# DeltaNet layer and two-level mixture of experts: chunks of 32 tokens instead of 64, the triangular inverses moved from TensorE to VectorE

## The chip, the core and the metric

The kernel runs on one core of one Trainium2 chip. The metric is the time of the whole program on the device, in microseconds (us); lower is better. Engines are named as in the profile: PE is TensorE (PEld its weight loads), DVE VectorE, ACT ScalarE, POOL GpSimd, SP the queue of SyncE, which issues most DMAs. Everything is fp32.

## What is computed

A DeltaNet layer of 4 batches x 8 heads over 768 tokens of width 48, and a mixture of 16 experts (4 groups of 4) on its result, read as 3072 tokens of width 384:

```python
k_n = k / (np.linalg.norm(k, axis=-1, keepdims=True) + 1e-06)
for t in range(S):                       # S = 768, per batch and head
    y[t] = q[t] @ state                  # state is 48 x 48
    v_old = state.T @ k_n[t]
    state = state + beta[t] * np.outer(k_n[t], v[t] - v_old)
x = y.transpose(0, 2, 1, 3).reshape(B * S, H * D)
g_idx, g_w = argmax and softmax weight of x @ w_group
e_idx, e_w = the same of x @ w_expert[g_idx]
out = (g_w * e_w)[:, None] * (np.maximum(x @ w1[g_idx, e_idx], 0) @ w2[g_idx, e_idx])
```

## The kernel before, in words

**Stage one, the DeltaNet.** The recurrence is cut into 12 chunks of 64 tokens. Two batches lie on the 128 partitions at a time (64 tokens each), so there are 24 units u, two for each chunk. For every chunk a unit lower triangular 64 x 64 matrix, made of the products of the chunk's keys with each other, has to be inverted for each batch and head: 384 matrices in all.

`prepare` (L186) does what needs no state. POOL scales the keys by their norms (L190) and the values (L193), PE turns the scaled keys (L198), ACT copies them (L200), PE forms the products keys x (keys, queries) into `g_ps` (L209), DVE masks them (L213, L218) and POOL makes three more operands of them (L222 to L225). Then the inverse is doubled up in five levels (loop at L231). Each level multiplies on PE into `y_ps` (L239), is masked by DVE (L242), is multiplied twice on PE into `m_ps` (L249, L251), and is copied by ACT (L261; L256 at the last level). Each of these products is 64 x 64 by 64 x 64; the two batches use opposite quarters of the PE array. An fp32 product leaves two records in the trace.

`advance` (L265) brings a unit through the recurrence: `a_ps` (keys x state, L273), `f` (values minus that, DVE, L278), `w_ps` (the inverse times f, L284), `w` (ACT copy, L287), `d_ps` (keys x w, L292), and the state `s_bd` in SBUF is added up by DVE (L299). `outputs` (L303) adds queries x state (L308) and masked products x w (L314) into `o_ps`, and ACT copies them to `x` (L318).

`route` (L345) takes the two units of a chunk: PE turns `x` (L350) and multiplies by the router's weights (L355), DVE and POOL find group, expert and weight in some 30 tiny operations, PE counts ranks (L389, L391), DVE makes one-hot tiles (L418, L421), PE multiplies them into `p_ps` (L423), and DVE adds this to `table` (L424). The rows of `x` go to `x_dram` by SP.

`norms` (L173) makes the norms of all keys from squares on POOL and sums on DVE, at the start. Buffers in PSUM come in pairs (`bufs=2`, L118). What runs when on each engine is decided by a planner from the order of the program text (loop at L427: the two units' `advance`, the next two units' `prepare`, then `route`).

**Stage two, the experts.** From `idx` (L444) POOL gathers the tokens of each expert from `x_dram`, PE multiplies by w1 (L481) and w2 (L488), and POOL scatters the rows to the result (L492). Weights arrive two experts ahead. The change leaves this stage alone.

## Time and profile before

| what | value |
|---|---|
| median of three runs | 1145.88 us (1144.49 to 1146.13) |
| the profiled execution, span from first to last instruction | 1145.2 us |
| busy: PE, PEld, DVE, ACT, POOL | 1026.7, 863.4, 316.1, 226.8, 245.5 us |
| busy shares of PE, PEld, DVE, ACT, POOL | 90%, 75%, 28%, 20%, 21% |
| granted clock of TensorE, mean of the span | 0.955 of 2.4 GHz |
| instructions in the profile | 35577 |

The profiled execution is one run; its own time is its span, and the page records nothing around it. A share of busy time is a mean over two stages with different limits, so the page is read by stage. The views used further down are a table of busy time by stretch (one row for each stretch: length, then busy us and number of instructions for each engine, granted clock, DMA share, GB/s), groups of instructions (line, engine, operation, tiles, shapes, count, then busy us and mean ns of one, then the idle time before them), and the timeline (start us, duration us, engine, line, operation). The clock is 1.00 where TensorE runs at 2.4 GHz and 0.50 where it runs at 1.2 GHz.

### The profile page before, as it was taken

What the parts mean: (1) busy time and instruction counts of PE and PEld (TensorE: products, weight loads), DVE (VectorE), ACT (ScalarE), POOL (GpSimd) and SP (SyncE); (2) the same over time, 40 slices, a digit from 0 to 9 for tenths busy, and PEclk for the clock granted to TensorE, in tenths of its full rate; (3) what the DMA queues carried; (4) which work ended last, traced back from release to release, by engine and by line L of the source; (5) the groups of instructions that cost most, each with busy time, mean ns of one, the idle gap of its engine ahead of it and who ended that gap; (6) DMA issues with size and microseconds to landing.
All of it is one profiled execution on the core that took longest, in us unless ns stands there. A gap on an engine that the chain in (4) does not pass through costs nothing. (4 is left out here: it accounts for less than half of the span.)

```text
span 1145.2 us, 35577 instructions
## 1 busy us (share of the span) xinstructions
PE 1026.7 (90%) x16298; PEld 863.4 (75%) x16298; DVE 316.1 (28%) x983; ACT 226.8 (20%) x429; POOL 245.5 (21%) x389
## 2 busy tenths in 40 slices
PE   0698999999999999998999999978999999999996
PEld 0587888888888887888888888866776677677674
DVE  4533434242423334242334242330100100110010
ACT  0132322222222222222222222210110011011000
POOL 5613122222222222122122221102211211221110
PEclk9999899999999999999999999988999999999998
DMA  9500100000100001010100000003545555464520
GB/s 297 209 11 10 31 17 23 23 24 17 30 17 21 26 17 30 10 30 17 31 9 17 16 17 2 17 16 107 190 146 191 165 185 173 165 199 141 192 68 11
DMA packets 41545, 83.49 MB, mean 73 GB/s; under 512 B 4377, under 2 KB 30156, under 8 KB 41394
## 3 DMA queue, kind: packets, MB, share of 16 engines
q1 hardware_dynamic: 33698, 65.30, 17.8%
q0 software_dynamic: 4096, 11.08, 2.9%
q10 hardware_dynamic: 3600, 4.82, 1.3%
q8 instruction: 128, 2.10, 0.8%
q14 instruction: 23, 0.19, 0.0%
HBM read 71.70 MB, written 11.06 MB: 72 GB/s over the span
## 5 line engine op out<-in xcount | busy, mean ns | idle before, releaser
L239 PE MATMUL y_ps<-mm,at 64*64 64x64 f32 x3840 | 227.7, 229 | 47.0 <-POOL mm L222 41.5
L251 PE MATMUL m_ps<-mm,y 64*64 64x64 f32 x3840 | 248.5, 228 | 0.2
L239 PEld LDWEIGHTS y_ps<-mm,at 64*64 64x64 f32 x3840 | 183.4, 140 | 69.3 <-POOL mm L222 51.9
L251 PEld LDWEIGHTS m_ps<-mm,y 64*64 64x64 f32 x3840 | 223.2, 143 | 2.4 <-DVE y L242 1.2
L249 PE MATMUL m_ps<-y,mm 64*64 64x64 f32 x3072 | 216.2, 233 | 1.3
L249 PEld LDWEIGHTS m_ps<-y,mm 64*64 64x64 f32 x3072 | 195.3, 142 | 16.0 <-DVE y L242 15.2
L242 DVE TENSOR_TENSOR y<-y_ps,con 128x256 f32<-128x256 f32 x240 | 101.8, 424 | 371.7 <-PE y_ps L239 368.7
L261 ACT ACTIVATE mm<-m_ps 128x512 f32<-128x512 f32 x192 | 114.7, 597 | 385.8 <-PE m_ps L251 385.8
L481 PE MATMUL h_ps<-xt,w 128*128 128x256 f32 x768 | 171.6, 384 | 8.1 <-DVE xt L475 8.1
L481 PEld LDWEIGHTS h_ps<-xt,w 128*128 128x128 f32 x768 | 145.9, 192 | 31.2 <-DVE xt L475 11.7
L488 PE MATMUL y_ps<-w,hid 128*128 128x384 f32 x512 | 167.7, 486 | 0.0
L488 PEld LDWEIGHTS y_ps<-w,hid 128*128 128x128 f32 x512 | 97.3, 190 | 64.4
L491 DVE TENSOR_SCALAR yo<-y_ps,xg 128x384 f32<-128x384 f32 x32 | 19.8, 618 | 321.0 <-PE y_ps L488 316.5
L484 ACT ACTIVATE hid<-h_ps 128x512 f32<-128x512 f32 x64 | 38.2, 597 | 322.3 <-PE h_ps L481 322.3
L492 POOL DMA_INDIRECT out_dram<-yo,idx x32 | 32.4, 1012 | 289.9 <-DVE yo L491 285.8
L190 POOL TENSOR_TENSOR kp<-k_all,rs 128x384 f32<-128x384 f32 x24 | 19.8, 829 | 303.9 <-PE g_ps L209 185.8
L209 PE MATMUL g_ps<-kqt 48*64 48x128 f32 x768 | 58.9, 284 | 0.7 <-ACT kqt L200 0.7
L224 POOL TENSOR_TENSOR at<-gq,con 128x256 f32<-128x256 f32 x48 | 34.9, 726 | 77.4 <-DVE gq L213 77.4
L198 PE MATMUL kt_ps<-con,kp 128*128 128x128 f32 x96 | 17.1, 300 | 36.4 <-POOL kp L190 34.8
L209 PEld LDWEIGHTS g_ps<-kqt 48*64 48x64 f32 x768 | 43.0, 137 | 2.3 <-ACT kqt L200 1.1
L284 PE MATMUL w_ps<-f,mt 64*64 64x48 f32 x704 | 43.0, 241 | 0.2 <-DVE f L278 0.2
L273 PE MATMUL a_ps<-s_bd,kqt 128*64 128x96 f32 x352 | 42.4, 262 | 0.0
(115 smaller groups left out, 922.2 us busy)
## 6 DMA issues: line engine op xcount, KB each, us to landing
w<-in_w_dram SPq DMA_DIRECT2D x32, 1536.0 KB, 6.8
x_dram<-x SPq DMA_DIRECT2D x48, 97.0 KB, 2.2
k_all<-in_k_dram ACTq DMA_DIRECT2D x24, 192.0 KB, 4.7
v<-in_v_dram SPq DMA_DIRECT2D x24, 192.0 KB, 2.5
kqt<-in_q_dram SPq DMA_DIRECT2D x48, 96.0 KB, 2.2
con<-in_const_dram SPq DMA_DIRECT2D x1, 708.5 KB, 5.2
xg<-x_dram,idx POOLq DMA_INDIRECT x32, 3.2
out_dram<-yo,idx POOLq DMA_INDIRECT x32, 3.3
```

The source lines that it names most:

```text
L209: nc.tensor.matmul(g_ps[halves[b], j], lhsT=kqt[rows, 0, j, t], rhs=kqt[rows, :, j, t], start=True, stop=True, skip_group_check=True)
L224: nc.gpsimd.tensor_tensor(at, gq[:, :, 0, :], eye, op=ALU.add)
L239: nc.tensor.matmul(y_ps[b, j], lhsT=at[b, j], rhs=mm[b, 0, j], start=True, stop=True, skip_group_check=True)
L242: nc.vector.tensor_tensor(y, y_ps, mask[:, None, :].to_broadcast([128, NP, C]), op=ALU.mult)
L249: nc.tensor.matmul(m_ps[b, 0, j], lhsT=mm[b, 1, j], rhs=y[b, j], start=True, stop=True, skip_group_check=True)
L251: nc.tensor.matmul(m_ps[b, 1, j], lhsT=y[b, j], rhs=mm[b, 1, j], start=True, stop=True, skip_group_check=True)
L261: nc.scalar.activation(new, m_ps, ACT.Copy)
L273: nc.tensor.matmul(a_ps[halves[b], 2 * j:2 * j + 2, :], lhsT=kqt[:, 0, j, halves[b]], rhs=s_bd[:, 2 * g + b, j], start=True, stop=True, sk ...
L284: nc.tensor.matmul(w_ps[b, h], lhsT=mts[h % 2][b, h // 2], rhs=f[b, h], start=True, stop=True, skip_group_check=True)
L481: nc.tensor.matmul(h_ps[:, k], lhsT=w1[:, j, (f + k) * 128:(f + k + 1) * 128], rhs=xt[:, j], start=(j == 0), stop=(j == DC - 1), skip_grou ...
L484: nc.scalar.activation(hid[:, f:f + 2], h_ps, ACT.Relu)
L488: nc.tensor.matmul(y_ps, lhsT=hid[:, f, i * 128:(i + 1) * 128], rhs=w2[:, f], start=(f == 0), stop=(f == FC - 1))
```

## The change

Chunks are 32 tokens long and all four batches lie on the partitions at once (4 x 32 = 128), so there are 24 chunks u in one chain. The changed functions:

- `gram(u)`: PE multiplies raw keys by (keys, queries) in 32 products; ACT copies the key part into `gt`, transposed for the inverse, and the query part into `gq`, which POOL masks. There is no key scaling and no PE turn of keys: keys arrive from HBM in both layouts (`kq`, `kv`).
- `inverse(g)`: for a group of four chunks, DVE transposes 32 x 32 blocks so that each of the 128 partitions holds one whole 32 x 32 matrix (4 chunks x 8 heads x 4 batches = 128). The norms are the root of its diagonal (ACT Ln and Exp). Then 30 column steps follow, j = 1 to 30, each two DVE instructions over (31 - j) x j elements; POOL scales before and after, and DVE transposes back to `mt`.
- `scale(u)`: POOL multiplies the values by the norms.
- `advance(u)`: as before with 32 x 32 inverses. The state stays in PSUM (`s_ps`, four banks), PE accumulates into it, and ACT copies it to `s_bd`.
- `logits(u)` and `route(r)`: the router's scores for each chunk, the rest for each four chunks.
- The order on PE, DVE, ACT and POOL is as written: `work(n)` gives n steps to each unfinished `inverse` and `route` between the parts of `advance`.
- PSUM has single buffers: 4 banks of state, 2 of `g` (`g_ps`, `r_ps`, `p_ps`), 1 of `s` (`a_ps`, `w_ps`, `t_ps`, `l_ps`), 1 of `o`. `norms`, `root` and the masks of the doubling are gone.

The core of the diff (the old `prepare` and `advance` are printed above):

```diff
-C = 64
-LEVELS = (2, 4, 8, 16, 32)
+C = 32
+RG = 4
+LEAD = 9
...
+ps = first.enter_context(tc.tile_pool(name="ps", bufs=1, space=PSUM))
+s_ps = ps.tile([128, B, 512], F32, tag="state", name="s_ps")
+NB, NV = LEAD + 3, 4
...
+def gram(u):
+    g, uu = divmod(u, RG)
+    kqt = kqt_[u % NB]
+    if uu == 0:
+        gts[g] = wk.tile([128, C, RG, H], F32, tag="gt", name=f"gt{g}")
+    g_ps = ps.tile([128, 2, 512], F32, tag="g", name=f"g_ps{u}")
+    g_out = g_ps[:, :, 0:NP * 2 * C].rearrange("p f (j a t) -> p f j a t", j=NP, a=2)
+    for j in range(NP):
+        for b in range(B):
+            for hh in range(2):
+                rows = slice(hh * 64, hh * 64 + D)
+                nc.tensor.matmul(g_out[quads[b], hh, j], lhsT=kqt[rows, 0, j, quads[b]],
+                                 rhs=kqt[rows, :, j, quads[b]], start=True, stop=True,
+                                 skip_group_check=True)
+    nc.scalar.activation(
+        gts[g][:, :, uu].rearrange("p t (f j) -> p f j t", f=2), g_out[:, :, :, 0, :],
+        ACT.Copy)
+    gq = wk.tile([128, 2, NP, C], F32, tag="gq", name=f"gq{u}", bufs=LEAD + 1)
+    nc.scalar.activation(gq, g_out[:, :, :, 1, :], ACT.Copy)
+    nc.gpsimd.tensor_tensor(
+        gq, gq, cut["upper"][:, None, None, :].to_broadcast([128, 2, NP, C]),
+        op=ALU.mult)
+    gqs[u] = gq
+def inverse(g):
+    m = wk.tile([128, C, C], F32, tag="m", name=f"m{g}")
+    nc.vector.transpose(out=m.rearrange("p i j -> p (i j)"),
+                        in_=gts.pop(g).rearrange("p t u h -> p (t u h)"))
+    yield
+    diag = m.rearrange("p i j -> p (i j)")[:, ::C + 1]
+    nrm, r0, r1 = [sm.tile([128, C], F32, tag=n, name=f"{n}{g}")
+                   for n in ("nrm", "r0", "r1")]
+    nc.vector.tensor_scalar(r0, diag, 1e-36, None, op0=ALU.max)
+    nc.scalar.activation(r0, r0, ACT.Ln)
+    nc.scalar.activation(r0, r0, ACT.Exp, scale=0.5)
+    yield
+    nc.vector.reciprocal(r1, r0)
+    yield
+    nc.vector.tensor_tensor(r1, r1, diag, op=ALU.mult)
+    nc.vector.tensor_tensor(r0, r0, r1, op=ALU.add)
+    nc.vector.tensor_scalar(nrm, r0, 0.5, 1e-6, op0=ALU.mult, op1=ALU.add)
+    yield
+    nc.vector.reciprocal(r1, nrm)
+    nc.vector.tensor_tensor(r0, r1, r1, op=ALU.mult)
+    nc.vector.tensor_tensor(r0, r0, bt[:, g], op=ALU.mult)
+    norm[g] = sm.tile([128, C], F32, tag="normt", name=f"normt{g}")
+    nc.vector.transpose(out=norm[g], in_=nrm)
+    nc.gpsimd.tensor_tensor(m, m, cut["below"].rearrange("p (i j) -> p i j", i=C),
+                            op=ALU.mult)
+    nc.gpsimd.tensor_tensor(m, m, r0[:, :, None].to_broadcast([128, C, C]), op=ALU.mult)
+    yield
+    yield
+    for j in range(1, C - 1):
+        n = C - 1 - j
+        t = wk.tile([128, C * C // 4], F32, tag="t", name=f"t{g}_{j}")
+        tv = t[:, 0:n * j].rearrange("p (i c) -> p i c", i=n)
+        nc.vector.tensor_tensor(tv, m[:, j + 1:, j:j + 1].to_broadcast([128, n, j]),
+                                m[:, j:j + 1, 0:j].to_broadcast([128, n, j]),
+                                op=ALU.mult)
+        nc.vector.tensor_tensor(m[:, j + 1:, 0:j], m[:, j + 1:, 0:j], tv, op=ALU.add)
+        yield
+    nc.gpsimd.memset(diag, 1.0)
+    nc.gpsimd.tensor_tensor(m, m, r0[:, None, :].to_broadcast([128, C, C]), op=ALU.mult)
+    yield
+    yield
+    mt = wk.tile([128, RG * H, C], F32, tag="mt", name=f"mt{g}")
+    nc.vector.transpose(out=mt.rearrange("p r i -> p i r"),
+                        in_=m.rearrange("p i j -> p (i j)"))
+    mts[g] = mt
...
+def advance(u):
+    g, uu = divmod(u, RG)
+    kqt, k, mt, f, gq = kqt_[u % NB], kv_[u % NV][:, 0], mts[g], vhs.pop(u), gqs.pop(u)
+    if u > 0:
+        a_ps = ps.tile([128, H, D], F32, tag="s", name=f"a_ps{u}")
+        for j in range(NP):
+            for b in range(B):
+                nc.tensor.matmul(a_ps[quads[b], 2 * j:2 * j + 2, :],
+                                 lhsT=kqt[:, 0, j, quads[b]], rhs=s_bd[:, b, j],
+                                 start=True, stop=True, skip_group_check=True)
+        vh, f = f, wk.tile([128, H, D], F32, tag="f", name=f"f{u}")
+        nc.vector.tensor_tensor(f, vh, a_ps, op=ALU.subtract)
+    o_ps = ps.tile([128, H, D], F32, tag="o", name=f"o_ps{u}")
+    if u > 0:
+        for j in range(NP):
+            for b in range(B):
+                nc.tensor.matmul(o_ps[quads[b], 2 * j:2 * j + 2, :],
+                                 lhsT=kqt[:, 1, j, quads[b]], rhs=s_bd[:, b, j],
+                                 start=(j == 0), stop=False, skip_group_check=True)
+    yield
+    w_ps = ps.tile([128, H, D], F32, tag="s", name=f"w_ps{u}")
+    for h in range(H):
+        for b in quads:
+            nc.tensor.matmul(w_ps[b, h], lhsT=mt[b, uu * H + (h % 2) * NP + h // 2],
+                             rhs=f[b, h], start=True, stop=True, skip_group_check=True)
+    w = wk.tile([128, H, D], F32, tag="w", name=f"w{u}")
+    nc.scalar.activation(w, w_ps, ACT.Copy)
+    yield
+    if u < NCH - 1:
+        for odd in range(2):
+            for j in range(NP):
+                for b in range(B):
+                    hh = (b + odd) % 2
+                    nc.tensor.matmul(s_at[hh * 64:hh * 64 + D, b, j],
+                                     lhsT=k[quads[b], 2 * j + hh],
+                                     rhs=w[quads[b], 2 * j + hh],
+                                     start=(u == 0 and j == 0), stop=True,
+                                     skip_group_check=True)
+        for hh in range(2):
+            rows = slice(hh * 64, hh * 64 + D)
+            nc.scalar.activation(s_bd[rows, :, :, hh, :], s_at[rows], ACT.Copy)
+    yield
+    for h in range(H):
+        for b in quads:
+            nc.tensor.matmul(o_ps[b, h], lhsT=gq[b, h % 2, h // 2], rhs=w[b, h],
+                             start=(u == 0 and h == 0), stop=True,
+                             skip_group_check=True)
+    x = wk.tile([128, XW], F32, tag="x", name=f"x{u}", bufs=7)
+    nc.scalar.activation(x[:, 0:DM], o_ps.rearrange("p h d -> p (h d)"), ACT.Copy)
+    xs[u] = x
...
+    r_ps = ps.tile([128, RG, NE], F32, tag="g", name=f"r_ps{r}")
+    nc.tensor.matmul(r_ps, lhsT=before, rhs=hotf, start=True, stop=False)
+    nc.tensor.matmul(r_ps, lhsT=ones, rhs=pre, start=False, stop=True)
...
+    p_ps = ps.tile([128, NE * NS], F32, tag="g", name=f"p_ps{r}")
+    for g in range(RG):
+        nc.tensor.matmul(p_ps, lhsT=cols[g], rhs=rows[g], start=(g == 0),
+                         stop=(g == RG - 1))
...
+def work(n):
+    for _ in range(n):
+        for task in list(behind):
+            if next(task, "end") == "end":
+                behind.remove(task)
...
+    first_inverse = inverse(0)
+    for step in range(LEAD - RG):
+        for _ in range(5):
+            next(first_inverse)
+        gram(RG + step)
+    run(first_inverse)
+    scale(0)
+    for u in range(NCH + 1):
+        if u < NCH and u % RG == RG - 1 and (u + 1) // RG + 1 <= NGR - 1 or u == 0:
+            behind.append(inverse((u + 1) // RG + 1 if u else 1))
+        if u < NCH:
+            step = advance(u)
+            next(step)
+        work(4)
+        if u < NCH:
+            next(step)
+        if u + LEAD < NCH:
+            gram(u + LEAD)
+        turned = logits(u - 1) if 0 <= u - 1 < NCH else iter([None])
+        next(turned)
+        work(3)
+        if u < NCH:
+            next(step)
+        run(turned)
+        if u < NCH:
+            next(step)
+        if u + 1 < NCH:
+            scale(u + 1)
+        work(3)
+        if u + NB < NCH:
+            load_kq(u + NB)
+        if u + NV < NCH:
+            load_kv(u + NV)
+        if (u - 1) % RG == RG - 1 and u >= 1:
+            behind.append(route((u - 1) // RG))
+        if u in (2, 3):
+            weights[u - 2] = load_expert(u - 2)
+    while behind:
+        work(1)
```

## Rows read from the trace of the kernel before

**Rows 1.** Busy time by stretch, the whole span; the first line names the columns.

```profile
core 0: us, PE busy (x) PEld busy (x) DVE busy (x) ACT busy (x) POOL busy (x), PEclk, DMA share, GB/s
0.00:40.00 40.00, 4.00 (x36) 3.20 (x36) 19.00 (x41) 2.35 (x4) 26.96 (x46) 1.00 0.88 304
40.00:760.00 720.00, 667.88 (x14866) 600.62 (x14866) 255.33 (x839) 185.33 (x358) 153.77 (x273) 0.95 0.08 22
760.00:772.44 12.44, 6.06 (x21) 4.45 (x20) 5.92 (x37) 0.91 (x3) 1.18 (x6) 0.61 0.14 33
772.44:1145.20 372.76, 348.70 (x1376) 255.11 (x1376) 35.88 (x70) 38.23 (x64) 63.63 (x64) 0.98 0.44 148
```

**Rows 2.** Groups of instructions, PE, two of the inverse's three kinds of product.

```profile
L251 PE MATMUL m_ps<-mm,y 64*64 64x64 f32 x3840 | 248.5, 228 | 0.2
L239 PE MATMUL y_ps<-mm,at 64*64 64x64 f32 x3840 | 227.7, 229 | 47.0 <-POOL mm L222 41.5 <-ACT mm L261 3.5
```

**Rows 3.** Timeline of PE, two stretches of stage one: start us, duration us, instructions merged.

```profile
141.13 0.87 PE L273 MATMUL a_ps<-s_bd,kqt 128*64 128x96 f32 x8
141.93 1.59 PE L209 MATMUL g_ps<-kqt 48*64 48x128 f32 x32
143.46 0.87 PE L273 MATMUL a_ps<-s_bd,kqt 128*64 128x96 f32 x8
...
715.47 0.33 PE L249 MATMUL m_ps<-y,mm 64*64 64x64 f32 x4
...
716.40 0.56 PE L239 MATMUL y_ps<-mm,at 64*64 64x64 f32 x10
```

**Rows 4.** Timeline, the last route: the last copy of x, then the last one-hot products.

```profile
758.91 0.49 ACT L318 ACTIVATE x<-o_ps 128x384 f32<-128x384 f32 x1 [1.76 <-PE o_ps L314]
...
768.91 2.90 PE L423 MATMUL p_ps<-row,col 128*128 128x384 f32 x4 [2.19 <-DVE row L421]
```

**Rows 5.** Groups of instructions by shape, DVE, two inputs: 384, 176 and 16 elements.

```profile
L278 DVE TENSOR_TENSOR f<-vh,a_ps 128x384 f32<-128x384 f32 x22 | 12.1, 550 | 14.5 <-PE a_ps L273 14.5
...
L182 DVE TENSOR_TENSOR rs<-rs,sb 128x176 f32<-128x176 f32 x1 | 0.3, 343 | 0.0
L167 DVE TENSOR_TENSOR rk<-rk,ssq 128x16 f32<-128x16 f32 x1 | 0.2, 169 | 0.0
```

**Rows 6.** Timeline of DVE, two small instructions, the second needing the first.

```profile
743.45 0.17 DVE L399 TENSOR_SCALAR rank_i<-rank_i 128x2 int32<-128x2 int32 x1
743.65 0.17 DVE L401 TENSOR_SCALAR rank_i<-rank_i 128x2 int32<-128x2 int32 x1
```

**Rows 7.** Timeline of POOL and DVE at 28.5 us.

```profile
28.54 0.87 POOL L176 TENSOR_TENSOR sq<-k_all 128x384 f32<-128x384 f32 x1 [1.38 <-DVE ssq L177]
28.64 0.80 DVE L168 TENSOR_TENSOR rs<-rk,rk 128x16 f32<-128x16 f32 x1
```

**Rows 8.** Groups of instructions, POOL, two inputs: 256 and 384 elements.

```profile
L224 POOL TENSOR_TENSOR at<-gq,con 128x256 f32<-128x256 f32 x48 | 34.9, 726 | 77.4 <-DVE gq L213 77.4
...
L190 POOL TENSOR_TENSOR kp<-k_all,rs 128x384 f32<-128x384 f32 x24 | 19.8, 829 | 303.9 <-PE g_ps L209 185.8 <-PE d_ps L292 113.3 <-DVE rs L182 4.8
```

**Rows 9.** Groups of instructions, ACT, copies out of PSUM: 512 and 256 elements.

```profile
L261 ACT ACTIVATE mm<-m_ps 128x512 f32<-128x512 f32 x192 | 114.7, 597 | 385.8 <-PE m_ps L251 385.8
...
L256 ACT ACTIVATE mt<-m_ps 128x256 f32<-128x256 f32 x48 | 18.4, 384 | 52.3 <-PE m_ps L251 51.0 <-PE y_ps L239 1.2
```

**Rows 10.** Groups of instructions, DVE, the memset of the state.

```profile
L153 DVE MEMSET s_bd<- 128x1536 f32 x1 | 1.3, 1338 | 1.1 <-PEq L565 1.1
```

**Rows 11.** DMA issues: engine, count, KB each, median us from issue to landing.

```profile
kqt<-in_q_dram SPq DMA_DIRECT2D x48, 96.0 KB, 2.2
```

**Rows 12.** Busy time by stretch, columns as in rows 1, around a change of clock.

```profile
144.90:148.30 3.40, 1.16 (x25) 0.90 (x24) 1.01 (x3) 0.60 (x1) 3.32 (x6) 1.00 0.00 0
148.30:151.70 3.40, 3.40 (x63) 3.40 (x64) 0.33 (x1) 0.60 (x1) 0.71 (x1) 0.51 0.23 63
165.40:168.80 3.40, 3.40 (x110) 3.33 (x107) 0.42 (x1) 0.77 (x2) 0.00 (x0) 1.00 0.20 58
```

More of the change, by code (lines that the diff above doesn't have):

```diff
@@ L33, in constants @@
         "ident": (p[:, None] == p[None, :]),
-        "upper": twice(np.concatenate([upper, upper], axis=1)),
-        "eye": twice(eye),
-        "low0": twice(-below(1).astype(np.float32)),
-        "up0": twice(eye - below(1).T),
-        "level": twice(np.concatenate([eye - below(s) for s in LEVELS], axis=1)),
+        "upper": np.concatenate([(i < k).astype(np.float32)] * n_batch, axis=0),
+        "below": np.tile(-(i > k).astype(np.float32).reshape(1, C * C), (128, 1)),
         "before": (p[:, None] < p[None, :]),
@@ L57, in deltanet_then_moe @@
     shape: tuple,
-    k_d: bass.AP,
-    v_d: bass.AP,
-    q_d: bass.AP,
+    kq_d: bass.AP,
+    kv_d: bass.AP,
     beta_d: bass.AP,
@@ L83, in deltanet_then_moe @@
     STATIC = -(-N // (NE * 128))
-    halves = [slice(0, 64), slice(64, 128)]
+    assert B * C == 128 and NCH % RG == 0
+    NGR = NCH // RG
+    quads = [slice(b * C, (b + 1) * C) for b in range(B)]
     cp = ctx.enter_context(tc.tile_pool(name="const", bufs=1))
@@ L152, in deltanet_then_moe @@
+        for u in range(NV):
+            load_kv(u)
         nc.sync.dma_start(out=wr, in_=wr_d)
@@ L265, in advance @@
[L265 to L281 removed]
+        gts, gqs, mts, norm, vhs, xs = {}, {}, {}, {}, {}, {}
@@ L301, in advance @@
-            return outputs(u, c, g, kqt, gqs, w)
-        def outputs(u, c, g, kqt, gqs, w):
-            o_ps = ps.tile([128, H, D], F32, tag="q", name=f"o_ps{u}")
-            if c > 0:
-                for b in range(2):
-                    for j in range(NP):
-                        nc.tensor.matmul(o_ps[halves[b], 2 * j:2 * j + 2, :],
-                                         lhsT=kqt[:, 1, j, halves[b]],
-                                         rhs=s_bd[:, 2 * g + b, j], start=(j == 0),
-                                         stop=False, skip_group_check=True)
+            yield
@@ L410, in route @@
             nc.vector.tensor_tensor(ex, ex, at[:, :, 1:2], op=ALU.add)
+            yield
             idv = small("idv", [1])
-            for g in range(NG):
-                nc.gpsimd.tensor_scalar(idv[:, g], cut["rowid"], float(2 * g * S + c * C), 1.0,
+            cols, rows = [], []
+            for g, u in enumerate(us):
+                nc.gpsimd.tensor_scalar(idv[:, g], cut["rowid"], float(u * C), 1.0,
                                         op0=ALU.add, op1=ALU.mult)
-            p_ps = ps.tile([128, NE * NS], F32, tag="g", name=f"p_ps{c}")
@@ L421, in route @@
                 nc.vector.tensor_scalar(row, cut["iota"], ex[:, g], idv[:, g],
                                         op0=ALU.is_equal, op1=ALU.mult)
-                nc.tensor.matmul(p_ps, lhsT=col, rhs=row, start=(g == 0), stop=(g == NG - 1))
-            nc.vector.tensor_tensor(table, p_ps, table, op=ALU.add)
-        made = [prepare(u) for u in range(NG)]
-        for c in range(NCH):
-            nxt = range((c + 1) * NG, min((c + 2) * NG, NU))
-            for u in nxt:
-                vs[u] = load_qv(u)
-            if c == 0:
-                norms(NG, NU, nc.gpsimd)
-            ahead = []
-            xs = []
-            for g in range(NG):
-                xs.append(advance(c * NG + g, made[g]))
-                if nxt:
-                    ahead.append(prepare(nxt[g]))
-            made = ahead
-            route(c, xs)
-            if c < 2:
-                weights[c] = load_expert(c)
+                cols.append(col)
@@ new lines, in route @@
+                rows.append(row)
+                yield
+            yield
+            p_ps = ps.tile([128, NE * NS], F32, tag="g", name=f"p_ps{r}")
+            for g in range(RG):
+                nc.tensor.matmul(p_ps, lhsT=cols[g], rhs=rows[g], start=(g == 0),
+                                 stop=(g == RG - 1))
+            nc.vector.tensor_tensor(table, p_ps, table, op=ALU.add)
+            yield
+        behind = []
+        def work(n):
[3 more added lines that the diff above has]
+                        behind.remove(task)
@@ new lines, in run @@
+        def run(task):
+            for _ in task:
+                pass
+        with tc.manual_schedule(engines={mybir.EngineType.PE, mybir.EngineType.DVE,
+                                         mybir.EngineType.Activation, mybir.EngineType.Pool}):
+            for u in range(RG):
+                gram(u)
+            first_inverse = inverse(0)
[37 more added lines that the diff above has]
+                work(1)
```

310 lines of the change are left out of this document (96 added, 214 removed).

## The prediction, made before the changed kernel had run

> **What bounds the kernel now.** I read the table of busy time by stretch first [rows 1]. It splits the span of 1145.2 us into a start of 40 us, the DeltaNet to 760, the last route to 772.44, and the experts, 372.76 us. In the DeltaNet PE is busy 668 of 720 us, DVE 255, ACT 185, POOL 154, and the DMA engines 8%; in the experts PE is busy 349 of 373. PE bounds both. The change leaves the experts alone, so I carry their 372.8 us over, and only the other 772.4 us can move.
>
> Next the groups of instructions: two of the three kinds of product in the inverse alone have 7680 of PE's 16298 records and 476 us [rows 2]. These leave. A mean duration there is latency, not cost, because products overlap; the cost is the distance between starts in the timeline [rows 3]. Thirty-two records of 64x64 products start within 0.93 us (715.47 to 716.40), 29 ns each, on two opposite quarters of the array. Thirty-two `g_ps` records of 128 columns take 1.53 us, 48 ns each, alternating between two column halves. Eight `a_ps` records, all in one column half, take 0.80 us, 100 ns each with the change of shape.
>
> **PE after the change.** One chunk has 32 products in `gram`, 16 for `a_ps`, 16 for the state part of `o_ps`, 32 each for `w_ps`, the state and the masked part: 160, or 320 records. Tiles of 32 have no row. If four tiles overlap as two did, the distance is 15 ns; if no better than in `g_ps`, 48. I take 29, the nearest by size: 9.3 us (4.8 to 15.4). The turn of x and the logits are 9 records on the full array, 1.0 us at the 100 ns of the widest products above. `p_ps` needs 8 records for each group of four chunks; four last 2.9 us in a stretch at a clock of 0.61 [rows 1, 4], 0.7 us each, so about 0.5 at a better clock: 1.0 us for each chunk. PE's sum is **11.3 us for each chunk** (6.8 to 17.4), against 668/24 = 28 now for the same tokens.
>
> **DVE after the change.** This is the new heavy load. A two-input instruction costs 169 ns at 16 elements, 343 at 176 and 550 at 384 [rows 5]: 0.16 us and 1.04 ns an element. One that needs its predecessor starts 0.20 us behind it where the predecessor lasts 0.17 [rows 6], so a dependent pair loses another 0.03 to 0.04. For one `inverse` (four chunks) the sum of (31 - j) x j over j = 1 to 30 is 4960, twice that 9920 elements: 10.3 us, plus 60 x 0.20 = 12.0, together 22.3. The two transposes of 1024 elements have no row; I take the two-input price, 1.2 us each, and twice that as the upper end. Nine small instructions for norms and scales, 0.23 each, give 2.1. Beside the inverse stand four `f` (2.2 us), four copies of logits (0.8) and the route: 5.9 us was the last stretch with a two-tile route and a few odd instructions [rows 1]; with four tiles I take 7.5. The sum is 37.3 us a group, 9.3 for each chunk.
>
> **POOL stands in DVE's way.** At 28.54 us POOL starts a 0.87 us product, and a 16-element DVE product that starts at 28.64 lasts 0.80 us instead of 0.17, ending with POOL's [rows 7]. Both inputs of that one lie in SBUF, as they do in every column step; `f`, with one input in PSUM, does not show it. POOL's products cost 0.73 us at 256 elements and 0.83 at 384 [rows 8], so 1.34 at 1024. A group has four masks, four `scale`, three 1024s and about 1.4 us of route: 11.7 us, 2.9 for each chunk. Some 27 of DVE's 37 us have both inputs in SBUF, so I add three quarters, 2.2 us (0 to 2.9).
>
> The Trainium skill, page "SBUF — State Buffer", section "SBUF: two separate sides", says that such an instruction and a POOL instruction hold a shared port pair by turns, each for its whole length. The trace agrees (0.80 us against 0.17). By the rule alone all 2.9 us would be added, and the sum below would be 13 us higher.
>
> **Waits in the written order.** `p_ps` holds PE for 4 us while DVE has only one column step before `table` needs it, about 2.5 us lost a group. Norms pass DVE, ACT, DVE and POOL in turn; two spare steps cover most, and I count 2.5 more. That is 1.2 us for each chunk (0 to 2.5), estimated. What is queued behind them on DVE is the next column step and then `f`, for which PE's `w_ps` waits.
>
> DVE's pace is then 9.3 + 2.2 + 1.2 = **12.7 us a chunk** (9.3 to 15). PE's 11.3 lie beside it. So does the chain of the state: `w_ps` 1.9, its copy hidden behind `gram` 1.9, state products 1.9, two state copies of 768 elements at 0.81 by the ACT prices [rows 9], `a_ps` 0.9, `f` 0.55, some 10 us with hand-overs. ACT has about 5 us a chunk and is hidden; so are the removed norms, masks and POOL's key scaling. SP issues seven DMAs a chunk. A row write waits there for its route, but loads run three chunks ahead for `kq`. The tightest is `kv` behind two experts' weights: 7 MB at the 304 GB/s of the first 40 us [rows 1] is 23 us, against some 30 us of lead. If that cover is gone, it is one wait of a few us.
>
> **The start.** `kq` buffers are cleared first and then loaded: 0.9 us for 1024 elements by the DVE memset [rows 10] after 1.1 us of idling, then a landing of 2.2 us [rows 11], so about 4.5 us. Four `gram` follow in series, since `g_ps` has one buffer: 1.9 + 2 x 0.384 + hand-overs = 3.0 each, to 16.5. Transpose, norms, ACT and two POOL products take 8: 24.5. The column steps take 22.3 and collide with five masks (3.6): 50.4. The last POOL product and transpose end at **54 us** (48 to 64). The 7.3 MB loaded meanwhile need 24 us at 304 GB/s and are hidden.
>
> **The end of stage one.** The inverses end with chunk 18, so 19 chunks run at 12.7 (241 us). The last five run at PE's 11.3 (57 us). From the last copy of x (758.91 + 0.49 [rows 4]) to 772.44 were 13.0 us; two more tiles add four `p_ps` records (2.9) and one-hot tiles (1.5, an estimate): 17.4.
>
> **The sum**: 54 + 241 + 57 + 17 + 372.8 = **742 us**, against 1145.2 of the profiled execution. That execution is 0.7 us under the median of 1145.88, inside the runs' spread, so I forecast the median as 742 too.
>
> **Rivals.**
> 1. *Small tiles pack well and POOL does not collide* (20%). For it: four quarters could run where two do. A chunk then costs DVE's 9.3 + 1.2 = 10.5, and 9 where the chain alone rules: 54 + 200 + 45 + 17 + 373 = 689. Against it: the 0.80 us of [rows 7].
> 2. *TensorE falls to 1.2 GHz* (20%). In 144.90 to 148.30 PE had 25 records and was busy 1.16 of 3.40 us at a clock of 1.00; the next stretch got 0.51, with 63 records where a full one has 110 [rows 12]. That is 54 ns a record for 31. Waiting for DVE could leave PE such gaps in every chunk. At 27 to 54 ns, with the 2 us of other products near 3.4, a chunk costs 12 to 20.6; in the middle, 16.5, the sum is 54 + 396 + 20 + 373 = 843.
> 3. *Slower than before* (3%). It needs more than (1145.2 - 54 - 17 - 373)/24 = 29 us a chunk. One mechanism could do it: tiles of 32 run one after another instead of side by side. Unpaired, `g_ps` would cost 96 ns for 128 columns at 2.4 GHz, so 96 for 64 columns and 72 for 48 at 1.2 GHz, and the 64 wide records twice 100: 64 x 200 + 64 x 96 + 192 x 72 ns = 32.7 us, with 3.4 of the rest 36, so 54 + 864 + 20 + 373 = 1311. Against it: `g_ps` pairs overlap, 48 ns against the 100 of single-file `a_ps` [rows 3].
> 4. *The order as written blocks* (5%): PE stands in its queue behind waits and the 10 us chain adds to DVE's load instead of lying beside it, some 20 us a chunk: 54 + 480 + 17 + 373 = 924.
>
> The forecast itself has 52%, from 700 to 790 by DVE's ends; less of it lies below, with rival 1. The range of 680 to 850 takes in the forecast, most of rival 1 and the lower half of rival 2. A measurement of this kernel can tell about 0.2% (2.3 us) from no change. All cases but rival 3 are far faster: 0.96, no change 0.01, slower 0.03.
>
> **What would show it.** Right: by stretch, DVE is busiest from about 54 us on and PE under 90%; 64 records in well under 2 us; column steps of some 0.2 to 0.4 us, longer where POOL runs; `idx` written near 370 us; the experts again 373 us. Wrong: idle time of DVE before `f` above 2 us a chunk (PE or the chain bounds); a granted clock near 0.5 (rival 2); column steps of even length beside POOL (rival 1); a start far above 64 us.

## The result, and the profile after

The changed kernel took 738.43 us in the median of four runs (737.15 to 740.53), the kernel before 1145.18 in the runs beside it: a ratio of 0.645, interval 0.6437 to 0.6463. The forecast was 742.0, its range 680 to 850. The profiled execution has a span of 737.4 us.

Busy time by stretch of the changed kernel, cut where the first `w_ps` begins, where the copy of w of chunk 19 begins, after the last copy of x, and where `idx` is written (columns as in [rows 1]):

```profile
core 0: us, PE busy (x) PEld busy (x) DVE busy (x) ACT busy (x) POOL busy (x), PEclk, DMA share, GB/s
0.00:58.40 58.40, 12.11 (x577) 9.16 (x578) 36.33 (x80) 12.82 (x24) 20.42 (x27) 1.00 0.64 161
58.40:307.40 249.00, 175.60 (x6098) 145.21 (x6098) 183.14 (x544) 83.66 (x152) 79.45 (x128) 0.73 0.29 83
307.40:347.10 39.70, 31.46 (x1145) 25.50 (x1145) 10.91 (x47) 14.11 (x25) 4.92 (x20) 0.91 0.13 34
347.10:365.40 18.30, 9.37 (x23) 5.50 (x23) 8.65 (x45) 0.92 (x3) 3.46 (x18) 0.53 0.17 43
365.40:737.40 372.00, 347.85 (x1376) 254.53 (x1376) 34.91 (x64) 38.22 (x64) 63.73 (x64) 0.98 0.44 149
```

These are the stages of the forecast's sum: start 58.4 (54 forecast), 19 chunks with an inverse beside them 249.0 (241), the last five 39.7 (57), end of stage one 18.3 (17.4), experts 372.0 (372.8). The total is 4.6 us under the forecast because a tail 17 us shorter pays for 12 us more in start and loop; that these errors cancel is luck. In the loop DVE is the busiest engine, as forecast, but it is idle for 26% of it, and PE's clock is 0.73.

Groups of the changed kernel by shape, between 60 and 347 us (line, engine, operation, tiles, count, then busy us and mean ns of one, then idle before):

```profile
L276 ACT ACTIVATE s_bd<-s_ps 48x768 f32<-48x768 f32 x46 | 37.0, 805 | 50.9 <-PE s_ps L269 50.2
...
L216 POOL TENSOR_TENSOR m<-m,r 128x1024 f32<-128x1024 f32 x5 | 11.8, 2353 | 5.2 <-DVE m L213 5.1
L201 POOL TENSOR_TENSOR m<-m,con 128x1024 f32<-128x1024 f32 x5 | 11.8, 2352 | 7.2 <-DVE r L192 7.2
...
L220 DVE STREAM_TRANSPOSE mt<-m 128x1024 f32<-128x1024 f32 x5 | 10.1, 2014 | 2.3 <-POOL m L216 2.3
L203 POOL TENSOR_TENSOR m<-m,r 128x1024 f32<-128x1024 f32 x5 | 9.6, 1911 | 2.5 <-DVE normt L200 1.6 <-DVE r L198 0.9
...
L198 DVE TENSOR_TENSOR r<-r,bt 128x32 f32<-128x32 f32 x5 | 7.2, 1440 | 0.2
...
L180 DVE STREAM_TRANSPOSE m<-gt 128x1024 f32<-128x1024 f32 x4 | 4.9, 1225 | 0.0
```

The state's copies cost what [rows 9] gave, 0.81 us. POOL's three products of 1024 elements cost 1.91 to 2.35 us where [rows 8] had been stretched to 1.34.

The timeline of the changed kernel, where one inverse hands over to the next:

```profile
203.41 0.88 PE L258 MATMUL w_ps<-f,mt 32*32 32x48 f32 x64 [0.68 <-DVE f L246]
...
204.80 1.28 ACT L187 ACT_TABLE_LOAD   x1 [3.17 <-DVE r L186]
...
206.34 1.28 ACT L188 ACT_TABLE_LOAD   x1
207.63 0.23 ACT L188 ACTIVATE r<-r 128x32 f32<-128x32 f32 x1
207.77 0.47 ACT L261 ACTIVATE w<-w_ps 128x384 f32<-128x384 f32 x1
207.90 0.35 DVE L190 RECIPROCAL r<-r 128x32 f32<-128x32 f32 x1 [3.17 <-ACT r L188]
...
209.73 2.35 POOL L201 TENSOR_TENSOR m<-m,con 128x1024 f32<-128x1024 f32 x1
209.85 2.27 DVE L198 TENSOR_TENSOR r<-r,bt 128x32 f32<-128x32 f32 x1
```

Four things stand there. Sixty-four records on 32-row tiles take 0.88 us from the first start to the last end, so they start at most 13.7 ns apart, where the forecast took the 29 of [rows 3]. At 209.85 a 32-element DVE product lasts 2.27 us beside POOL's 2.35, the collision of [rows 7] at three times the size. DVE waits 3.17 us for the root. And w, whose product was done at 204.3, is copied only at 207.77: the copy stands behind two table loads in ACT's queue.

Waits of DVE in the changed kernel, over its whole span (for what, us in total, times, longest):

```profile
DVE lg L333 <- PE l_ps L331: 44.1, 15, 4.9
DVE r L190 <- ACT r L188: 16.1, 6, 3.5
...
DVE t L210 <- POOL m L203: 9.8, 5, 2.0
DVE f L246 <- PE a_ps L242: 9.1, 9, 2.1
DVE col L410 <- PE p_ps L421: 7.9, 6, 2.7
...
DVE mt L220 <- POOL m L216: 4.8, 5, 2.5
```

The largest one, 44.1 us at the copy of the logits, has no term in the forecast. Half of it lies behind the loop, where DVE has little else to do. Between 60 and 300 us three of these lines read:

```profile
DVE lg L333 <- PE l_ps L331: 21.4, 8, 4.3
...
DVE f L246 <- PE a_ps L242: 2.5, 5, 1.7
DVE mt L220 <- POOL m L216: 1.7, 3, 0.6
```

The same thing seen from PE and ACT, in one chunk with u % 4 = 1 (timeline):

```profile
175.16 1.50 PE L258 MATMUL w_ps<-f,mt 32*32 32x48 f32 x64
...
179.56 0.22 ACT L307 ACTIVATE ex<-ex 128x16 f32<-128x16 f32 x1 [3.62 <-DVE ex L306]
...
179.68 0.47 ACT L261 ACTIVATE w<-w_ps 128x384 f32<-128x384 f32 x1
...
180.21 0.90 PE L324 MATMUL t_ps<-con,x 128*128 128x128 f32 x3 [2.71 <-ACT w L261]
...
182.31 0.69 PE L381 MATMUL r_ps<-hot,con 128*128 128x64 f32 x2 [1.20 <-POOL hot L361]
...
184.46 0.69 PE L382 MATMUL r_ps<-pre,con 128*128 128x64 f32 x2 [1.46 <-POOL pre L367]
```

w_ps is done at 176.66. Its copy waits 3.0 us behind the router's exponential, which waits for a DVE instruction queued among column steps. The state's products, ready to run at 180.15, begin at 185.08, behind `r_ps`, which waits for POOL twice. In a clean chunk (u = 19, with no `gram` and no column steps beside it) the copy starts 0.07 us and the products 0.5 us after what they need, and the chunk takes 7.3 us; this one took 16.7.

### The profile page after: what moved, and what is told of

The parts are those of the page before. It is cut to its first block, busy times and chain, and to the rows that moved or that the text cites. A ratio compares the mean times of both kernels' runs of the same rounds, so it can differ in the third digit from the quotient of the medians.

```text
span 737.4 us, 20571 instructions
## 1 busy us (share of the span) xinstructions
PE 576.4 (78%) x9218; PEld 439.9 (60%) x9218; DVE 273.9 (37%) x779; ACT 149.7 (20%) x267; POOL 172.0 (23%) x257
## 5 line engine op out<-in xcount | busy, mean ns | idle before, releaser
L213 DVE TENSOR_TENSOR m<-m,t 128x30 f32<-128x30 f32 (+9 forms) x180 | 71.4, 397 | 6.2
L210 DVE TENSOR_TENSOR t<-m 128x30 f32<-128x30 f32 (+9 forms) x180 | 65.2, 362 | 13.1 <-POOL m L203 9.8
L162 PE MATMUL g_ps<-kqt 48*32 48x64 f32 x1536 | 27.8, 277 | 28.0 <-issue 10.3
L276 ACT ACTIVATE s_bd<-s_ps 48x768 f32<-48x768 f32 x46 | 37.0, 805 | 50.9 <-PE s_ps L269 50.2
L242 PE MATMUL a_ps<-s_bd,kqt 128*32 128x96 f32 x736 | 29.6, 315 | 15.2 <-DVE lg L333 12.6
L162 PEld LDWEIGHTS g_ps<-kqt 48*32 48x32 f32 x1536 | 21.4, 133 | 32.7 <-issue 16.7
L258 PE MATMUL w_ps<-f,mt 32*32 32x48 f32 x1472 | 26.1, 231 | 12.4 <-DVE f L246 12.2
L502 POOL DMA_INDIRECT xg<-x_dram,idx x32 | 31.3, 979 | 18.9 <-DVE idx L485 9.5
L258 PEld LDWEIGHTS w_ps<-f,mt 32*32 32x32 f32 x1472 | 22.4, 127 | 18.2 <-DVE f L246 16.1
L280 PE MATMUL o_ps<-w,gq 32*32 32x48 f32 x1536 | 28.8, 239 | 2.1 <-issue 2.1
L331 PE MATMUL l_ps<-wr,xt 128*128 128x20 f32 x144 | 26.9, 319 | 2.8 <-issue 1.5
```

Source lines behind the costliest of these rows:

```text
L162: nc.tensor.matmul(g_out[quads[b], hh, j], lhsT=kqt[rows, 0, j, quads[b]], rhs=kqt[rows, :, j, quads[b]], start=True, stop=True, skip_grou ...
L210: nc.vector.tensor_tensor(tv, m[:, j + 1:, j:j + 1].to_broadcast([128, n, j]), m[:, j:j + 1, 0:j].to_broadcast([128, n, j]), op=ALU.mult)
L213: nc.vector.tensor_tensor(m[:, j + 1:, 0:j], m[:, j + 1:, 0:j], tv, op=ALU.add)
L242: nc.tensor.matmul(a_ps[quads[b], 2 * j:2 * j + 2, :], lhsT=kqt[:, 0, j, quads[b]], rhs=s_bd[:, b, j], start=True, stop=True, skip_group_c ...
L258: nc.tensor.matmul(w_ps[b, h], lhsT=mt[b, uu * H + (h % 2) * NP + h // 2], rhs=f[b, h], start=True, stop=True, skip_group_check=True)
L276: nc.scalar.activation(s_bd[rows, :, :, hh, :], s_at[rows], ACT.Copy)
```

## The experiments

The first pair of theories was D: DVE's load with its collisions sets the pace, and Q: the chain of the state (`a_ps`, `f`, `w_ps`, copy, state products, two copies) is held up in queues. R, S and T came later. The ratio is to the kernel before, measured beside each run. "Pace" is the mean time of a chunk between the starts of `a_ps` of chunks 5 and 17, read from each trace; DVE is its busy time between 100 and 300 us, where it was read.

| run | us | ratio (interval) | pace | DVE |
|---|---|---|---|---|
| the changed kernel | 738.4 | 0.645 (0.6437 to 0.6463) | 13.26 | 147.2 |
| e1 w first | 742.3 | 0.6478 (0.646 to 0.6495) | 13.26 | |
| e2 w and state first | 735.9 | 0.6425 (0.6409 to 0.6441) | 12.97 | |
| e3 mask three times | 761.4 | 0.6653 (0.6637 to 0.6668) | 14.31 | |
| e4 half the columns | 710.5 | 0.6219 (0.6194 to 0.6244) | 12.27 | 106.6 |
| e5 logits' copy on ACT | 738.1 | 0.6461 (0.6435 to 0.6487) | 13.02 | |
| e6 e5 and e2 | 734.4 | 0.6422 (0.6398 to 0.6447) | 12.85 | |
| e7 planner's order | 727.7 | 0.635 (0.6334 to 0.6366) | 12.47 | 147.5 |
| e8 e4 and e6 | 699.1 | 0.6107 (0.6092 to 0.6122) | 11.44 | 113.2 |
| e9 inverse begun early | 745.7 | 0.6506 (0.6481 to 0.6531) | 13.20 | |
| e10 e9, Newton, e5 | 725.2 | 0.633 (0.6307 to 0.6352) | 11.98 | |
| e11 route drawn apart | 725.7 | 0.6341 (0.6312 to 0.637) | 12.38 | 165.1 |
| e12 e11, Newton, e5 | 720.6 | 0.6297 (0.6283 to 0.631) | 11.91 | 168.7 |

### Moving the chain ahead (e1, e2)

`work(4)` is four rounds of column steps and route. e1 moves w_ps and the copy ahead of it; e2 also moves the state's products ahead of `work(3)`.

```diff
                 if u < NCH:
                     step = advance(u)
                     next(step)
+                    next(step)
                 work(4)
-                if u < NCH:
-                    next(step)
```

> The copy of w is written ahead of the four steps of work, so it no longer stands on ACT behind the Ln, Exp and router exponentials that wait for DVE. Theory Q (the chain of the state is held up in the queues; in the changed kernel the copy of w waits 3.0 to 4.1 us behind them in eight chunks, 29 us in all): 705 to 722 us. Theory D (DVE's load with POOL's collisions sets the pace, as forecast): 733 to 742 us, the waits only move.

> As e1, and the state products with their two copies are also written ahead of the three middle steps of work, in front of the ranks and one-hot products that make them wait 4 to 5 us in every second chunk. Theory Q: 680 to 705 us. Theory D: 733 to 742 us.

Measured: e1 742.3 and e2 735.9, 2.5 us less than the changed kernel, both with intervals that overlap its own: D's figures. In e1 the copy's wait is gone (under 0.1 us in every chunk), but in chunks with u % 4 = 1 the state's products then begin 8 us after the copy where they began 4.9 us after it, still behind `r_ps`. In e2 the time comes back as 3 to 5 us ahead of the next `a_ps`. Shifting the chain among the waits only changes where it waits.

### Load on POOL and on DVE (e3, e4)

```diff
+            for _ in range(3):
                 nc.gpsimd.tensor_tensor(
                     gq, gq, cut["upper"][:, None, None, :].to_broadcast([128, 2, NP, C]),
                     op=ALU.mult)
```

> POOL multiplies each gq by the 0/1 mask three times instead of once: the result is the same, POOL has 2 x 0.79 us more in each of 24 chunks, 38 us in all, with both inputs in SBUF. Theory D: DVE is held by most of it, 758 us or more. Theory Q: DVE has some 27% of idle time to absorb it, under 748 us.

Measured 761.4, 23 us more: D's figure, but only in part for D's reason. The column steps' excess over the shortest instruction of the same shape rose from 20.8 to 29.1 us in all, so collisions carry a third of it. Another 5.4 us came at the start (the first w_ps at 63.8 us, not 58.4), and some through POOL's queue: in chunks with u % 4 = 1 the state's products began 6.4 us after w and not 4.9, since `r_ps` waits for POOL.

```diff
             for j in range(1, C - 1):
+                if j % 2 == 0:
+                    yield
+                    continue
                 n = C - 1 - j
```

> The column steps with even j are left out (their part of the inverse is not computed), the order of all else stays: DVE loses some 10 us of each of six inverses. Both theories lose 10 us at the start. Theory D: five more times 10, so 675 to 690 us. Theory Q: in the loop only what of the waits is DVE's own steps ahead of the exponentials, 695 to 722 us.

Measured 710.5: 69 us of column steps left out (136.6 to 67.3 us), 28 us gained. At the start nearly all of it pays (10.8 us for one inverse of six); in the loop 18.6 us are gained for some 58 left out. DVE's busy time between 100 and 300 us fell from 147.15 to 106.64:

```profile
100.00:300.00 200.00, 149.16 (x5370) 122.59 (x5357) 106.64 (x357) 72.53 (x132) 63.47 (x134) 0.79 0.25 66
```

DVE is idle for 47% of that stretch: D alone is refuted, the measurement lies in Q's range. But Q's own moves had given nothing in e1 and 2.5 us in e2. Hence theory R, a ring in which each engine waits in turn for another.

### The largest wait (e5, e6)

```diff
-            nc.vector.tensor_copy(lg_[r][:, g], l_ps)
+            nc.scalar.activation(lg_[r][:, g], l_ps, ACT.Copy)
```

> The logits' copy out of PSUM goes from VectorE to ScalarE, nothing else. In the changed kernel it is the largest wait of VectorE: 44.1 us behind l_ps in 15 of the copies, about 1.8 us a chunk. Theory D (VectorE's load, collisions with POOL and its waits set the pace): VectorE loses neither the copy (0.2 us x 24 = 5) nor most of its wait, so 30 to 45 us go: 695 to 710 us. Theory Q (the chain of the state is held up in queues): that wait lies beside the chain, VectorE arrives earlier at its next wait, and only the next a_ps, which shares the PSUM bank with l_ps, comes free sooner: 725 to 738 us. Theory R (a ring of waits in the written order, each engine waiting in turn for another): part of the wait reappears at f, at the column tiles or at the inverse's transposed tile: 712 to 728 us.

Measured 738.1, the upper edge of Q's range: nothing, for the removal of DVE's largest wait (21.4 us of it in this stretch). Waits of DVE in this run, 60 to 300 us:

```profile
DVE f L246 <- PE a_ps L242: 13.5, 6, 2.9
DVE r L190 <- ACT r L188: 12.2, 4, 3.2
DVE t L210 <- POOL m L203: 7.9, 4, 2.0
DVE mt L220 <- POOL m L216: 7.2, 4, 1.8
```

In the same stretch the changed kernel had 2.5 us at `f` and 1.7 at `mt`: DVE arrived sooner and waited at the next instruction. The wait at the copy was a symptom of a late PE, not a price.

> The logits' copy on ScalarE, and also w_ps with its copy ahead of four column steps, and the state's products ahead of the other three, as in the earlier run of both moves alone (735.9 us). There the time saved behind the copy came back as a wait of 3 to 5 us ahead of the next a_ps, which waited for the logits' copy on VectorE. Theory Q: with that wait gone the moves pay in full, 2 to 3 us a chunk in three chunks of four: 680 to 700 us. Theory D: the moves give nothing beside the copy: within 5 us of the run with the copy alone. Theory R: a few us below the run with the copy alone, 700 to 715 us.

Measured 734.4, 3.7 us under e5: D's figure, within 5 us of e5, and far from Q's 680 to 700 and R's 700 to 715. The place of `w_ps` and the state's products in the order isn't what holds it. Theory S, told with e8, keeps both bounds.

### The written order itself (e7)

```diff
-        with tc.manual_schedule(engines={mybir.EngineType.PE, mybir.EngineType.DVE,
-                                         mybir.EngineType.Activation, mybir.EngineType.Pool}):
+        with ExitStack():
```

> The written order is taken away: the scheduler of the language orders the four engines' instructions again, the work is the same. If the engines' loads set the pace (theory D), any order that keeps VectorE fed gives about the same: 730 to 770 us. If the order of the queues does (Q, R), a planner that doesn't know what waits for what loses the overlap of chain and column steps in part: 780 to 924 us, the upper end being the prediction's fourth rival, 20 us a chunk with the chain of 10 us added to VectorE's load.

Measured 727.7, under both expectations: the planner's order of the same work is 10.8 us faster than the written one, with the same busy time of DVE (147.47 against 147.15). So this part of the change cost time. By stage, the planner loses 10 us at the start (the first w_ps at 68.1 us, not 58.4) and gains 18 in the loop, where all but three copies of w come within 0.1 us of w_ps. Which of its placements gives the gain isn't shown: e1 had that copy on time too and gained nothing.

### Both loads at once (e8)

The edits of e4 and e6 together, and

```diff
-                col = wk.tile([128, 128], F32, tag="col", name=f"col{u}", bufs=2)
+                col = wk.tile([128, 128], F32, tag="col", name=f"col{u}", bufs=4)
-                row = wk.tile([128, NE * NS], F32, tag="row", name=f"row{u}", bufs=3)
+                row = wk.tile([128, NE * NS], F32, tag="row", name=f"row{u}", bufs=4)
```

> Both loads are cut at once: the column steps with an even column left out (so that part of the inverse isn't computed), as in the earlier run with half the column steps (710.5 us), and the logits' copy on ScalarE with w_ps and the state's products moved ahead, as in the run before this (734.4 us), and four buffers each for the one-hot tiles. Theory S (two bounds close to each other: VectorE's stream, 9.5 us busy a chunk and some 3 of waits, and just under it the chain of the state with its queues, 12 us a chunk): either cut alone finds the other bound, both together go well beyond their sum of 28 + 4 us: 665 to 690 us. Theory D (VectorE alone): no more than the sum, 700 to 710 us. Theory Q (the queues alone): the half columns add nothing that the order didn't, 710 to 725 us.

Measured 699.1, 11.4 us under e4, where the order alone had given 4.0. That is more than the sum, as S has it, but S wanted 665 to 690, and the four buffers are a third edit that neither e4 nor e6 had. Between 60 and 300 us DVE waited 7.8 us for `col` in e4 and 8.8 in e6, and not at all in e8, so the buffers alone may be the difference: the run doesn't show that the two cuts help each other. In this run DVE waits 46.4 us for `a_ps` between 60 and 300 us, so the chain rules, and chunks with u % 4 = 1 still take 13 to 14 us. What holds them had not been touched yet: the route.

### Covering the inverse's waits (e9, e10)

```diff
-                if u < NCH and u % RG == RG - 1 and (u + 1) // RG + 1 <= NGR - 1 or u == 0:
-                    behind.append(inverse((u + 1) // RG + 1 if u else 1))
+                if u == 0:
+                    behind.append(inverse(1))
...
+                if u % RG == RG - 2 and (u + 2) // RG + 1 <= NGR - 1:
+                    behind.append(inverse((u + 2) // RG + 1))
                 turned = logits(u - 1) if 0 <= u - 1 < NCH else iter([None])
```

> The inverse of the next group but one is appended in the middle of a chunk with u % 4 = 2 and not at the start of u % 4 = 3, so that the last column steps of one inverse and the first steps of the next stand side by side in the written order. Nothing else moves, and no work is added. Inside one inverse VectorE waits three times: 2.7 us for ScalarE's root (r L190), 1.6 for POOL before the first column step (t L210) and about 1 to 1.8 for POOL before the transposed tile (mt L220); with two inverses side by side a column step of the other one stands in those places. Theory S: these 5 to 6 us a group, five groups, go in part from the pace: 712 to 728 us. Theory Q: nothing, or some loss where twice the column steps stand ahead of f in two chunks of four: 735 to 750 us. Theory D with load and collisions alone, without waits: the same, 735 to 740 us.

Measured 745.7, 7 us more: Q's figure. DVE still waits 13.8 us for the root. In chunks with u % 4 = 2 `f` now comes 2.4 us late, behind two streams of steps, and the state's copies 2.9 us late, behind the table loads of Ln and Exp in ACT's queue; the chunks with u % 4 = 3 regain that, so the pace is unchanged (13.20). The time is lost outside the chunks of the pace: 4 us in the first five and 2 in chunk 18.

e10 adds e5, the four buffers, and this in place of Ln and Exp:

```diff
-            nc.scalar.activation(r0, r0, ACT.Ln)
-            nc.scalar.activation(r0, r0, ACT.Exp, scale=0.5)
+            nc.vector.tensor_scalar(r1.bitcast(I32), r0.bitcast(I32), 1, None,
+                                    op0=ALU.arith_shift_right)
+            nc.vector.tensor_scalar(r0.bitcast(I32), r1.bitcast(I32), 532487669, None,
+                                    op0=ALU.add)
```

(a Newton step more follows before the one that was there).

> All that could help together, in the changed kernel's order of chain and columns: the inverse begun early, the logits' copy on ScalarE, four buffers for the one-hot tiles, and the root of the norms by two Newton steps from a shifted exponent on VectorE instead of Ln and Exp on ScalarE, which takes away the wait r L190 and four table loads of 1.28 us in each group from ScalarE's queue and adds six small VectorE instructions, 1.2 us a group. Theory S: 695 to 715 us. Theory Q: only the table loads' share of the w copy's wait, 3.5 us in a chunk out of four, 715 to 730 us. Theory D: 735 to 745 us.

Measured 725.2, 20.5 us under e9 and inside Q's 715 to 730, not S's. Three edits came at once here, so the run doesn't say which of them gave it. Chunks with u % 4 = 1 still took 16 to 17.5 us, which points to the route: theory T.

### The route drawn apart (e11)

```diff
+            yield
             ed = weight_end(*exs)
...
+            yield
+            yield
             yield
             r_ps = ps.tile([128, RG, NE], F32, tag="g", name=f"r_ps{r}")
```

and each exponential, and the first weight's sum, one step later.

> The changed kernel with the route's steps drawn apart, nothing else: each of its two exponentials is issued one step behind the subtraction that it needs, the weights' sums one step later, and r_ps three steps later, so that it falls behind the masked products of its chunk and p_ps behind those of the next. No work is added. Theory T: what holds the chain in chunks with u % 4 = 1 and 2 is the route's own waits, standing in the queues of PE (r_ps waits for POOL, then p_ps, ahead of the state's products: 4.7 us in each of the two chunks where a clean chunk has 0.5) and of ScalarE (an exponential that waits for VectorE ahead of the copy of w: 3.5 us). These two chunks lose up to 10 us a group, until VectorE's stream (9.5 us busy a chunk, and 6 us of waits inside the inverse a group, so 44 of the present 51.6 us) sets the pace: 710 to 722 us. Theory S with VectorE as the first bound: 730 to 738 us. Theory Q as first put, where only the order of the chain's own instructions counts: no change, 735 to 740 us.

Measured 725.7, 12.7 us less with no work added or removed: not far above T's 710 to 722, and under the 730 to 738 of S. The timeline of the same chunk (u = 9) in this run:

```profile
172.79 0.88 PE L258 MATMUL w_ps<-f,mt 32*32 32x48 f32 x64
...
173.74 0.49 ACT L261 ACTIVATE w<-w_ps 128x384 f32<-128x384 f32 x1
...
176.23 0.42 PE L162 MATMUL g_ps<-kqt 48*32 48x64 f32 x4 [1.80 <-issue]
...
177.42 1.32 PE L269 MATMUL s_ps<-w,kv 32*48 32x48 f32 x64
...
181.50 0.69 PE L385 MATMUL r_ps<-hot,con 128*128 128x64 f32 x2
...
182.45 0.69 PE L386 MATMUL r_ps<-pre,con 128*128 128x64 f32 x2 [0.26 <-POOL pre L368]
```

w is copied 0.07 us after w_ps, and `r_ps` runs behind the state's products, hardly waiting. The chunk took 13.2 us, not 16.7; the pace fell by 0.9 us a chunk, and DVE's busy time in the 200 us rose from 147 to 165. The waits of DVE in this run, 60 to 300 us, show the one for `l_ps` gone:

```profile
DVE r L190 <- ACT r L188: 14.3, 5, 3.5
DVE t L210 <- POOL m L203: 7.9, 4, 2.0
DVE col L414 <- PE p_ps L425: 4.7, 4, 2.1
DVE f L246 <- PE a_ps L242: 4.5, 9, 2.0
```

`r_ps` waits for POOL as long as before (10.0 us in that stretch, 9.9 before), but no longer ahead of the chain. Part of the gain is given back: the next chunk (u = 10) takes 13.5 us, not 12.0, since its `a_ps` waits for the copy of the logits, which stands behind the one-hot tiles. The moves on ACT's queue and on PE's weren't run apart. The 1.80 us of "issue" ahead of 176.23 have no releaser in the trace and stay unexplained; the changed kernel has such gaps too, 10.3 us in all ahead of `g_ps`.

### All of it (e12)

The edits of e11, the Newton root, e5 and the four buffers; the inverse begins where it did.

> The last run's route drawn apart (725.7 us), and with it what else takes a wait out of a queue: the root of the norms by two Newton steps on VectorE in place of Ln and Exp (no wait r L190, and no table loads ahead of the copy of w in chunks with u % 4 = 3, which still waits 3.5 us there), the logits' copy on ScalarE (VectorE doesn't wait for l_ps, nor a_ps for VectorE), four buffers for the one-hot tiles. Against the run with the inverse begun early (725.2 us), that part is left as in the changed kernel, since alone it cost 7 us. Theory T (the waits of route and norms in the queues were the chain's delay, and VectorE's stream is the bound just under it): 20 to 25 us less than 725.7 if the queues still ruled, but VectorE's stream, 9.5 us a chunk and 1.2 for the Newton steps and 4 for POOL's two products a group, allows no less than 43 to 46 us for four chunks against 49 now: 700 to 712 us. If VectorE's stream rules already: 718 to 726 us.

Measured 720.6, the fastest version that computes everything: 17.9 us under the changed kernel, 425 under the kernel before. It fell in the case "VectorE's stream rules already". Busy time between 100 and 300 us, and two instructions of DVE's timeline:

```profile
100.00:300.00 200.00, 146.64 (x5330) 121.07 (x5325) 168.67 (x471) 64.84 (x135) 69.75 (x119) 0.79 0.27 76
```

```profile
186.34 0.28 DVE L420 TENSOR_SCALAR col<-con,at 128x128 f32<-128x128 f32 x1
186.53 2.60 DVE L423 TENSOR_SCALAR row<-con,ex,idv 128x384 f32<-128x384 f32 x1
```

DVE is now busy for 84% of the stretch, and part of that is the collision again: POOL's 2.35 us product, started at 186.57, holds a one-hot tile that takes 0.47 us alone. The mean of these tiles is 1179 ns here, 474 in the changed kernel. Tightening the order moved the collision to another instruction.

## Why the prediction was right

The forecast's likeliest case came true: DVE is the busiest engine, and a chunk takes 13.1 us (249.0 / 19) where 12.7 was forecast. That the figure is so near is luck in part. Its three terms were off in both directions: DVE's load 8.7 for 9.3, collisions 1.5 for 2.2, waits 2.8 for 1.2.

**DVE's load: nearly right.** 183.14 / 19 = 9.6 us a chunk with collisions. Of these 183.14 us, 28.7 are what DVE's instructions in the loop last beyond the shortest of their own shape, the collisions. The rest, with 11.3 us of gaps under 0.15 us between instructions, which the forecast had counted here, is 8.7 a chunk. Dependent pairs lose what [rows 6] said: a column step of 228 elements starts 0.44 us behind its partner (117.08 and 117.52), as 0.16 + 0.24 + 0.04 gives.

**"POOL stands in DVE's way", 2.2 us a chunk: mis-sized, 1.5.** Of the 28.7 us, the column steps lose 17.9, L198 6.2 and L194 2.0. Single collisions are as long as forecast or longer (L198 lasts 2.27 us in three inverses of six, 0.19 in the others), but fewer instructions meet one: POOL was busy 79.45 us in the loop, and DVE lost a good third of that, where the forecast counted three quarters of 2.9 us a chunk. POOL's price of 1024 elements, 1.34, was mis-sized too. The Trainium skill, page "GPSIMD Engine Reference", section "3.1 Elementwise — side-by-side cycle accounting", has 4497 ns for a two-input add of 2048 elements; half of that, 2.25 as an estimate, is near the 2.35 of L201 and L216, so there the page was the better price than two small rows drawn out.

**"Waits in the written order", 1.2 us a chunk (0 to 2.5): the step that failed.** DVE's waits in the loop are 53.5 us, 2.8 a chunk. The forecast's two items, `p_ps` and the norms, are 28.6 of them, 1.5 a chunk. What it left out is the other direction, 25.0 us at `lg` and `f`, where DVE waits for PE: it looked at what holds DVE, and not at the route's instructions in PE's and ACT's queues ahead of the chain. e11 shows that: 12.7 us for moving them alone, with the wait at `lg` gone. The forecast's own sign for a late chain, idle time before `f`, stayed small (2.5 us), because DVE met the late PE at the copy of the logits first.

**"The chain is hidden": half wrong.** Undisturbed (u = 19) it takes 7.3 us; the forecast's 10 are 8 without the 1.9 of `gram`, which that chunk doesn't have. With the queues it is about as long as DVE's stream: fewer column steps (e4) brought the pace from 13.26 to 12.27, and there the chain held; the route drawn apart (e11) brought it to 12.38, with DVE busy for 83% of the time. So two bounds seem to lie within about a microsecond of each other; no run cut both and nothing else. Rival 4 (5%) named a mechanism of this kind, and was oversized at 20 us a chunk.

**PE, 29 ns a record: mis-sized, at most 13.7 at 2.4 GHz.** Thirty-two-row tiles pack at half the distance of [rows 3], the lower bound given (15). So PE was busy 9.2 us a chunk at a clock of 0.73, not 11.3. Half of rival 1 came true (tiles pack), its other half did not.

**The last five chunks, 57 us: 39.7, the largest miss of the sum.** The forecast put them at PE's 11.3, but `gram` runs nine chunks ahead, so 64 of the 320 records aren't in them, and PE was busy for 31.46 of the 39.70 us.

**Rival 2's clock** came true in part (0.73, with DVE's waits in between). Groups of `w_ps`, state and `a_ps` take 1.5, 1.3 and 1.5 us at 1.2 GHz against 0.9 each; over chunks 1 to 18 that adds about 0.9 us a chunk to the chain (an estimate from these durations). How much of it other waits hide isn't shown. In e11 the same estimate gives 0.9, so that run's gain isn't the clock's.

**The start, 54: 4.4 short.** The first keys were there at 8.2 us, not 4.5: their load was issued at 1.98 us, behind those of beta and constants (0.75 and 1.21), and a load of 192 KB lands after 6.6 us in the median, against 2.2 for 96 KB in [rows 11]. Which of the two made it late isn't shown. Behind that the first transpose starts after 12.1 us, at 20.3 (12.0 forecast), again because two errors cancel: a `gram` takes 2.1 us and not 3.0, but the fourth stands still for 2.8 us ahead of 18.76 with no releaser in the trace. The first w_ps comes 38.1 us later (37.5).

## What to carry to other kernels

Where several streams of work are written into one order by hand, read each queue for instructions of a side stream that wait for another engine ahead of the main chain; moving those a few steps later added no work here and gained 12.7 us. A wait that goes without the time falling was a symptom: look for who made the late engine late. When two bounds are close, cutting one gains only as far as the other (e4: 18.6 of some 58 us in the loop), and a run that cuts both should change nothing else.
